# FFN bias rows of a fused attention and FFN kernel: loaded at the start and turned into columns among the first key transposes

## The chip, the cores and the metric

One Trainium2 chip, one of its cores. The metric is the device time in microseconds (us) of one execution. All runs used here are of the fast state, with a granted TensorE clock of 1.0 (in the kernel before and the changed one it is lower only past 1235 us, when PE has finished). The engines are called PE (TensorE, with PEld for its weight loads), DVE (VectorE), ACT (ScalarE), POOL (GpSimd) and SP (SyncE).

## The reference, cut to what matters

```python
xn = _layernorm(A_x)                                   # 2048 rows of 512
s  = attention(xn @ wq, k_cache, v_cache) @ wo         # 32 heads, 2048 keys of 128
h  = jnp.einsum("bsd,df->bsf", xn, w1) + b1            # F = 1792; b1 is the bias of this change
g  = silu(relu(h)**2 @ w2 + b2)
out = A_x + s * g
```

The kernel computes `h` transposed, with the 1792 features on the partitions: 14 chunks of 128. The bias must then be a column for each chunk, a tile `b1f` of 128 x 14, while it lies in memory as 14 rows of 128.

## The kernel before

Each engine has its own list of instructions, which wait on semaphores; in the traces here it starts them in the order of its list (an example: in k_late_keys_changed below the bias rows land near 6.3 us, but their transpose stands behind the keys and starts at 7.60 us). PE does in each step (there are 8 to a head and block of 512 queries, 1024 in all) two score matmuls into `psA`, one to three "fillers" into `psF`, and eight weighted-value matmuls into `psO`. Fillers are the matmuls of everything else: query projections, FFN, output projection. A filler job is a chain of matmuls that accumulate in one bank; two banks take turns, and a job's bank is free when DVE has evacuated it:

```python
(n, mm, evac), i = cur[0]
bank = bank_no[0]
mm(i, bank)                               # waits for t_bankF[bank] at i == 0
if i == n - 1:
    t_bankF[bank] = evac(bank, step)      # DVE reads the bank
    bank_no[0] ^= 1                       # the next job takes the other bank
```

All jobs are chains of 4 to 16 matmuls, save one: the bias job, a single transpose of 14 rows on PE, with its copy on DVE.

```python
def mm(n, bank):
    box[0] = E(PE, partial(_peT, out=bankF(bank)[:, 0:64].bitcast(BF16)[:, 0:NFC], in_=b1b[:],
                           ident=ident[0:NFC, 0:NFC]), deps=[tok_b1, t_ident, t_bankF[bank]])
def evac(bank, step):
    t_b1[0] = E(DV, partial(_copy, out=b1f[:], in_=...), deps=[box[0]])
    return t_b1[0]
return 1, mm, evac
...
jobs = [(3, 3, job_b1(), None)]           # sorted in behind projections 1 and 2
```

The first head is special: its keys arrive as rows and are transposed on PE, in halves `b`, and its query rows come in four blocks `i`. The order of emission at the start (each engine takes its own instructions from it, in this order):

```python
k0_transpose(0); k0_copy(0); ...; ln_scale(0, 0)
first_transpose(0)     # PE: normalised rows of block 0
k0_transpose(1)        # PE: second half of the keys
k0_copy(1); ...        # ACT
first_copy(0)          # DVE: xnT
first_proj(0)          # PE
ln_scale(0, 1)         # DVE: xn_t of block 1
first_evac(0)          # DVE: qt_sb
first_transpose(1)     # PE
gen_scores(0)          # PE: the first scores
```

The softmax here doesn't subtract the row's maximum and nothing guards it: scores larger than these inputs give would overflow.

Of the kernel before, what the change touches and what calls it, by code (L numbers as in the profile page):

```python
# [7 lines left out]
BF16 = mybir.dt.bfloat16  # L8
F32 = mybir.dt.float32
P = 128  # L10
# [204 lines left out]
def bass_recurrent_scan__mha_block_cached__dense_activation_squared_relu__prompt_kernel(  # L215
# [23 lines left out]
    NFC = F // P  # L239
# [12 lines left out]
    S = _Sched()  # L252
    PE = S.eng("PE")
    AC = S.eng("ACT")
    DV = S.eng("DVE")
    GP = S.eng("POOL")
    SP = S.eng("SP")
    E = S.emit
# [22 lines left out]
    b1b = sb("b1b", [NFC, P], BF16)  # L281
    b1f = sb("b1f", [P, NFC], F32)
# [8 lines left out]
    ident = sb("ident", [P, P], BF16)  # L291
# [7 lines left out]
    psA = nc.alloc_psum_tensor("psA", [P, 4 * 512], F32)  # L299
# [3 lines left out]
    def bankF(i):  # L303
        return psF[:, i * 512:(i + 1) * 512]

    def bankO(i):
        return psO[:, i * 512:(i + 1) * 512]
# [10 lines left out]
    sl_b1 = S.slot("b1")  # L318
# [10 lines left out]
    t_ident = E(GP, partial(_ts, out=ident[:], in0=identf[:], scalar1=0.0, scalar2=None,  # L329
                            op0=ALU.is_equal), deps=[t_idf])  # L330
    t_ones = None
    for i in range(NSL):
        t_ones = E(GP, partial(_memset, out=v_sb[:, i, :, Dh:Dh + 1], val=1.0))


    t_xl = {}
    t_xn = {}
# [18 lines left out]
    def ln_rstd(j, i, n=1, eng=GP):  # L356
        jt = j * TPB + i
        prev = [t_xn.get(jt - TPB), t_xr.get(jt - TPB)]
        t = E(DV, partial(_bn_aggr, out=mv_t[:, i, :], in_=st_t[:, i, 0:6 * n]),
              deps=[t_bn[jt]] + prev)  # L360
        t = E(eng, partial(_ts, out=ve_t[:, i:i + 1], in0=mv_t[:, i, 1:2], scalar1=1.0,
                           scalar2=LN_EPS, op0=ALU.mult, op1=ALU.add), deps=[t] + prev)
        t_xr[jt] = E(GP, partial(_tt, out=rstd[:, i:i + 1], in0=ve_t[:, i:i + 1], in1=mhalf[:],
                                 op=ALU.pow), deps=[t, t_mhalf])
# [5 lines left out]
    def ln_scale(j, i):  # L370
        jt = j * TPB + i
        t_xn[jt] = E(DV, partial(_ts, out=xn_t[:, i, :], in0=x_ln[:, i, :],
                                 scalar1=mv_t[:, i, 0:1], scalar2=rstd[:, i:i + 1],
                                 op0=ALU.subtract, op1=ALU.mult),
                     deps=[t_xr[jt], t_xnr.get(jt - TPB)])
# [12 lines left out]
    t_k0 = [None, None]  # L388
    t_kT0 = [None, None]
    t_q0 = [None] * TPB  # L390
# [21 lines left out]
    def k0_transpose(b):  # L412
        n = NKT // 2
        for c in range(n):
            t_kT0[b] = E(PE, partial(_peT, out=bankO(b).bitcast(BF16)[:, c * P:(c + 1) * P],
                                     in_=kT[:, NSL - 1, (b * n + c) * P:(b * n + c + 1) * P],
                                     ident=ident[:]),
                         deps=[t_k0[b], t_ident], inc=(c == n - 1))

    def k0_copy(b):  # L420
        n = NKT // 2 * P
        t_k0[b] = E(AC, partial(_act, out=kT[:, 0, b * n:(b + 1) * n],
                                in_=bankO(b).bitcast(BF16), func=ACT.Copy), deps=[t_kT0[b]])

    def first_transpose(i):
        for c in range(NDC):
            t_xT[i] = E(PE, partial(_peT, out=bankF(1)[:, 0:256].bitcast(BF16)[:, c * P:(c + 1) * P],
                                    in_=xn_t[:, i, c * P:(c + 1) * P], ident=ident[:]),
                        deps=[t_xn[i], t_ident, tok_xT[0][i - 1] if i else None],
                        inc=(c == NDC - 1))  # L430
        t_xnr[i] = t_xT[i]

    def first_copy(i):
        tok_xT[0][i] = E(
            DV, partial(_copy, out=xnT[:, :, i * P:(i + 1) * P],
                        in_=bankF(1)[:, 0:256].bitcast(BF16).rearrange("p (c q) -> p c q", q=P)),
            deps=[t_xT[i]])

    def first_proj(i):
        for c in range(NDC):  # L440
            t_proj[0] = E(PE, partial(_mm, out=bankF(0)[:, i * P:(i + 1) * P],
                                      lhsT=wq_sb[:, 0, c, :], rhs=xnT[:, c, i * P:(i + 1) * P],
                                      start=(c == 0), stop=(c == NDC - 1)),
                          deps=[t_wqfill[0], tok_xT[0][i], t_q0[i - 1] if i else None],
                          inc=(c == NDC - 1))
# [21 lines left out]
    t_exp = [None] * NPAIR  # L467
# [36 lines left out]
    def gen_scores(pi):  # L504
        g, k = divmod(pi, NPR)
        s2, i = pi % 2, g % NSL
        assert t_kfill[g] is not None and t_evac[g] is not None
        t = None
        if g == 0:
            qt, b = divmod(pi, 2)  # L510
            for c in range(NKT // 2):
                t = E(PE, partial(_mm_shared, out=psA[:, s2 * 1024 + c * P:s2 * 1024 + (c + 1) * P],
                                  lhsT=kT[:, 0, (b * NKT // 2 + c) * P:(b * NKT // 2 + c + 1) * P],
                                  rhs=qt_sb[:, 0, qt * P:(qt + 1) * P], start=True, stop=True),
                      deps=[t_k0[b], t_q0[qt], t_exp[pi - 2] if pi >= 2 else None],
                      inc=(c == NKT // 2 - 1))
        else:
            for n in range(2):
                tt = 2 * k + n
                t = E(PE, partial(_mm, out=psA[:, s2 * 1024 + n * 512:s2 * 1024 + (n + 1) * 512],  # L520
                                  lhsT=kT[:, i, tt * P:(tt + 1) * P], rhs=qt_sb[:, g % NQS, :],
                                  start=True, stop=True),
                      deps=[t_exp[pi - 2] if pi >= 2 else None, t_kfill[g], t_evac[g],
                            t_bankF[0] if pi == 0 else None],
                      inc=(n == 1))
        if k == NPR - 1:
            t_S_last[g] = t
        t_exp[pi] = E(AC, partial(_act, out=pT[:, pi % NPT, :],
                                  in_=psA[:, s2 * 1024:(s2 + 1) * 1024],
                                  func=ACT.Exp, scale=SM_SCALE),  # L530
                      deps=[t, t_PV[pi - NPT] if pi >= NPT else None])
# [51 lines left out]
    t_bankF = [None, None]  # L583
# [19 lines left out]
    def at(step, fn):  # L603
        events.setdefault(step, []).append(fn)

    def job_proj(g):
# [14 lines left out]
                          deps=[t_proj[g], t_S_last[g - NQS] if g >= NQS else None])  # L621
            return t_evac[g]
        return NDC, mm, evac

    t_b1 = [None]

    def job_b1():

        box = [None]

        def mm(n, bank):
            box[0] = E(PE, partial(_peT, out=bankF(bank)[:, 0:64].bitcast(BF16)[:, 0:NFC],
                                   in_=b1b[:], ident=ident[0:NFC, 0:NFC]),
                       deps=[tok_b1, t_ident, t_bankF[bank]])

        def evac(bank, step):
            t_b1[0] = E(DV, partial(_copy, out=b1f[:],
                                    in_=bankF(bank)[:, 0:64].bitcast(BF16)[:, 0:NFC]),
                        deps=[box[0]])
            return t_b1[0]  # L640
        return 1, mm, evac

    def job_h(j, c):
        js = slice(j * QB, (j + 1) * QB)
# [119 lines left out]
                                op=ALU.add), deps=[t, tok_xt[jt]])  # L764


    jobs = [(3, 3, job_b1(), None)]
    for g in range(1, NG):
        jobs.append((NPR * g - 15, NPR * (g - 2), job_proj(g), g))
    for j in range(NQB):  # L770
        b = 30 + j * (SPB - 6)
# [92 lines left out]
    load_w1(0)  # L864
    for i, k in enumerate([2, 3, 12, 18, 26, 34]):
        at(k, partial(load_w1, i + 1))
    tok_b1 = tok_b2 = None

    def load_b1():
        nonlocal tok_b1  # L870
        tok_b1 = S.emit_dma(GP, partial(_dma, out=b1b[:],
                                        in_=B_b1.rearrange("(c p) -> c p", p=P)), sl_b1)

    def load_b2():
        nonlocal tok_b2
# [33 lines left out]
    ln_scale(0, 0)  # L909
    first_transpose(0)  # L910
    k0_transpose(1)
    k0_copy(1)
    t_kfill[0] = t_k0[1]
    ln_rstd(0, 1, eng=DV)
    first_copy(0)
    first_proj(0)
    ln_scale(0, 1)
    first_evac(0)
    first_transpose(1)
    gen_scores(0)  # L920
    ln_bn(0, 2)
    gen_scores(1)
    first_copy(1)
    ln_rstd(0, 2)
    first_proj(1)
    first_evac(1)
    gen_pv(0)
    ln_bn(0, 3, 0, HD)
    gen_scores(2)
    ln_scale(0, 2)  # L930
    first_transpose(2)
    ln_bn(0, 3, HD, D)
    gen_scores(3)
    first_copy(2)
    ln_rstd(0, 3, n=2)
    load_b1()
    first_proj(2)
    first_evac(2)
    gen_pv(1)
# [22 lines left out]
    for pi in range(NPAIR):  # L962
# [4 lines left out]
        n = 0  # L967
# [31 lines left out]
    step = NPAIR  # L999
# [41 lines left out]
```

## Time and profile before

| | before |
|---|---|
| median of three runs | 1239.27 us (1239.21 to 1239.27) |
| span of the profiled run | 1237.5 us |
| PE, ACT, DVE busy | 99%, 85%, 38% |
| waits of PE in the list | 2.0 us, of which 0.4 after the first 20 us |
| bias rows: load issued, used | 12.09 us, 20.40 us |

PE sets the time; its busy share is an upper view, since its records overlap (a 512-column matmul has a record of 0.38 us, but the next starts 0.22 us later). So this document reads starts, not busy sums. Some matmul records are also missing from this trace: PE has 11666 records and PEld 11873, so a small gap in the list of PE isn't always idle time. The lines are shown in the prediction.

### The profile page before, as it was taken

The numbers are of one execution on the slowest core, as the hardware profiler recorded it, in microseconds if no ns is written. First come the engines' busy times: TensorE is split into PE (matmuls) and PEld (weight loads), VectorE is DVE, ScalarE is ACT, GpSimd is POOL, SyncE is SP. The second block draws the span as 40 slices with busy tenths as digits, with TensorE's granted clock in tenths as the row PEclk, the third lists the DMA queues.
The fourth block names the chain that finished last, engine by engine and source line by source line (L and its number), as shares of the span: only waits on it lengthen the run. The fifth ranks groups of instructions, "written<-read, shape, count | busy, mean of one in ns | idle before, by whom it ended". The sixth has DMA issues, their size and how long they took to land.

```text
span 1237.5 us, 26703 instructions
## 1 busy us (share of the span) xinstructions
PE 1221.4 (99%) x11666; PEld 818.6 (66%) x11873; DVE 472.9 (38%) x953; ACT 1053.6 (85%) x1044; POOL 32.0 (3%) x73
## 2 busy tenths in 40 slices
PE   9999999999999999999999999999999999999998
PEld 7666666666666666666666666666666666666666
DVE  4453333244435332334444532233344333324333
ACT  7888888888888888888888888888888888888885
POOL 1010000000002000000000200000000000000000
PEclk9999999999999999999999999999999999999999
DMA  9999988777888787877788888787788788778761
GB/s 209 217 235 180 191 178 140 128 139 140 144 154 166 143 161 133 133 141 146 135 132 169 171 141 142 137 150 137 133 145 149 147 154 157 138 134 146 146 123 31
DMA packets 686868, 185.41 MB, mean 150 GB/s; under 512 B 673536, under 2 KB 685568, under 8 KB 686752
## 3 DMA queue, kind: packets, MB, share of 16 engines
q1 hardware_dynamic: 684656, 179.62, 80.7%
q0 software_dynamic: 1424, 3.81, 1.1%
q8 instruction: 94, 1.54, 0.5%
q10 hardware_dynamic: 672, 0.26, 0.1%
q14 instruction: 22, 0.18, 0.1%
HBM read 96.60 MB, written 2.10 MB: 80 GB/s over the span
## 4 chain that ended last, share of the span: by engine, by line
PE 98%; issue 1%; DVE 1%; DMA 0%; ACT 0%; POOL 0%; DVEq 0%
PE psO L157 38%; PE psA L152 35%; PE psF L152 25%; PE psA L157 0%; DMA x_ln<-in_A_x_dram 0%; DVE out_t L165 0%; PE psF L196 0%; DVE tmp_t L175 0%; ACT pT L161 0%; DVE xnT L179 0%; DVE st_t L200 0%; DVE o_bf L165 0%; DVE qt_sb L179 0%; POOL rstd L165 0%; DVE o_un L179 0%
## 5 line engine op out<-in xcount | busy, mean ns | idle before, releaser
L161 ACT ACTIVATE pT<-psA 128x1024 bf16<-128x1024 f32 x1024 | 1043.6, 1023 | 165.0 <-PE psA L152 119.7
L157 PEld LDWEIGHTS psO<-v_sb,pT 128*128 128x128 bf16 x8192 | 547.9, 98 | 240.8 <-issue 13.1
L157 PE MATMUL psO<-v_sb,pT 128*128 128x129 bf16 x8192 | 631.2, 220 | 0.9 <-ACT pT L161 0.4
L152 PE MATMUL psA<-qt_sb,kT 128*128 128x512 bf16 x1837 | 562.3, 379 | 10.2
L179 DVE COPY o_un<-psO 128x258 f32<-128x258 f32 x256 | 97.4, 422 | 398.5 <-PE psO L157 397.7
L152 PE MATMUL psF<-xnT,wq_sb 128*128 128x512 bf16 (+1 forms) x514 | 167.1, 374 | 0.8 <-DVE b1f L179 0.4
L152 PE MATMUL psF<-wo_all,oT 128*128 128x512 bf16 x479 | 163.4, 379 | 0.1
L152 PEld LDWEIGHTS psA<-qt_sb,kT 128*128 128x128 bf16 x2032 | 156.9, 98 | 0.1
L179 DVE CAST qt_sb<-psF 128x512 bf16<-128x512 f32 (+1 forms) x131 | 88.7, 677 | 103.7 <-PE psF L152 98.0
L152 PEld LDWEIGHTS psF<-xnT,wq_sb 128*128 128x128 bf16 x524 | 50.6, 98 | 60.8 <-issue 1.2
L165 DVE TENSOR_TENSOR o_bf<-o_un,rden 128x512 bf16<-128x512 f32 x128 | 88.5, 692 | 4.7 <-DVE rden L183 0.3
L171 DVE TENSOR_SCALAR r_t<-psF,b1f 128x512 bf16<-128x512 f32 x56 | 42.0, 750 | 116.9 <-PE psF L152 116.9
L152 PEld LDWEIGHTS psF<-wo_all,oT 128*128 128x128 bf16 x480 | 46.9, 98 | 56.4
L152 PE MATMUL psF<-xnT,w_sb 128*128 128x512 bf16 x224 | 77.1, 379 | 0.0
L152 PE MATMUL psF<-w_sb,h2T 128*128 128x512 bf16 x223 | 73.7, 379 | 0.0
L152 PEld LDWEIGHTS psF<-w_sb,h2T 128*128 128x128 bf16 x224 | 21.9, 98 | 26.4
L152 PEld LDWEIGHTS psF<-xnT,w_sb 128*128 128x128 bf16 x224 | 21.9, 98 | 26.4
L165 DVE TENSOR_TENSOR z_t<-psF,b2bc 128x512 f32<-128x512 f32 x16 | 11.1, 692 | 68.3 <-PE psF L152 63.8
L165 DVE TENSOR_TENSOR acc<-psF,acc 128x512 f32<-128x512 f32 x28 | 19.3, 689 | 30.0 <-PE psF L152 30.0
L208 POOL DMA_DIRECT2D out_dram<-out_t x12 | 6.7, 554 | 890.4 <-DVE out_t L165 890.4
L183 DVE RECIPROCAL rden<-o_un 128x4 f32<-128x4 f32 x128 | 22.9, 179 | 4.4
L165 DVE TENSOR_TENSOR h2T<-r_t 128x512 bf16<-128x512 bf16 x56 | 23.8, 425 | 1.9
(44 smaller groups left out, 162.2 us busy)
## 6 DMA issues: line engine op xcount, KB each, us to landing
v_sb<-in_A_v_cache_dram SPq DMA_DIRECT2D x127, 512.0 KB, 4.7
wq_sb<-in_A_wq_dram SPq DMA_DIRECT2D x127, 128.0 KB, 3.4
wo_all<-in_A_wo_dram SPq DMA_DIRECT2D x4, 1024.0 KB, 6.3
w_sb<-in_B_w_dram SPq DMA_DIRECT2D x14, 256.0 KB, 5.1
oT<-o_bf SPq DMA_TRANSPOSE x128, 4.0
x_t<-in_A_x_dram POOLq DMA_DIRECT2D x16, 128.0 KB, 3.2
kT<-in_A_k_cache_dram SPq DMA_TRANSPOSE x127, 4.5
x_ln<-in_A_x_dram SPq DMA_DIRECT2D x15, 128.0 KB, 3.7
```

The lines of the kernel that those rows point to most:

```text
L152: return e.matmul(out, lhsT, rhs, start=start, stop=stop)
L157: return e.matmul(out, lhsT, rhs, start=start, stop=stop, skip_group_check=True)
L161: return e.activation(out, in_, func, bias=bias, scale=scale)
L165: return e.tensor_tensor(out, in0, in1, op)
L171: return e.tensor_scalar(out, in0, scalar1=scalar1, scalar2=scalar2, op0=op0, op1=op1)
L179: return e.tensor_copy(out, in_)
L183: return e.reciprocal(out, in_)
L208: return e.dma_start(out, in_)
```

## The change

The intent is to take the bias job out of the fillers. The rows are loaded at the very beginning; PE transposes them behind the second half of the first keys; DVE copies the columns before it normalises the second block of rows. The target moves from a filler bank to the last bank of `psA`, which the first scores of the kernel then have to leave alone until the copy is done.

```diff
     for i in range(NSL):
         t_ones = E(GP, partial(_memset, out=v_sb[:, i, :, Dh:Dh + 1], val=1.0))
+    tok_b1 = S.emit_dma(GP, partial(_dma, out=b1b[:], in_=B_b1.rearrange("(c p) -> c p", p=P)),
+                        sl_b1)
...
+    def bias_rows():
+        t_b1[0] = E(PE, partial(_peT, out=psA[:, 1536:1600].bitcast(BF16)[:, 0:NFC], in_=b1b[:],
+                                ident=ident[0:NFC, 0:NFC]), deps=[tok_b1, t_ident])
+    def bias_copy():
+        t_b1[0] = E(DV, partial(_copy, out=b1f[:], in_=...), deps=[t_b1[0]])
...
-                      deps=[t_k0[b], t_q0[qt], t_exp[pi - 2] if pi >= 2 else None],
+                      deps=[t_k0[b], t_q0[qt], t_exp[pi - 2] if pi >= 2 else t_b1[0]],
...
-    def job_b1():            # cut: shown above
-    jobs = [(3, 3, job_b1(), None)]
+    jobs = []
...
     k0_transpose(1)
+    bias_rows()
     k0_copy(1)
     ...
     first_copy(0)
+    bias_copy()
     first_proj(0)
     ln_scale(0, 1)
...
-    load_b1()                # was issued behind the fourth block's statistics
```

More of the change, by code (lines that the diff above doesn't have):

```diff
@@ L437, in first_copy @@
             deps=[t_xT[i]])
+    t_b1 = [None]
+    def bias_rows():
+        t_b1[0] = E(PE, partial(_peT, out=psA[:, 1536:1600].bitcast(BF16)[:, 0:NFC], in_=b1b[:],
+                                ident=ident[0:NFC, 0:NFC]), deps=[tok_b1, t_ident])
+    def bias_copy():
+        t_b1[0] = E(DV, partial(_copy, out=b1f[:],
+                                in_=psA[:, 1536:1600].bitcast(BF16)[:, 0:NFC]), deps=[t_b1[0]])
     def first_proj(i):
@@ L623, in job_proj @@
         return NDC, mm, evac
-    t_b1 = [None]
-    def job_b1():
-        box = [None]
-        def mm(n, bank):
-            box[0] = E(PE, partial(_peT, out=bankF(bank)[:, 0:64].bitcast(BF16)[:, 0:NFC],
-                                   in_=b1b[:], ident=ident[0:NFC, 0:NFC]),
-                       deps=[tok_b1, t_ident, t_bankF[bank]])
-        def evac(bank, step):
-            t_b1[0] = E(DV, partial(_copy, out=b1f[:],
-                                    in_=bankF(bank)[:, 0:64].bitcast(BF16)[:, 0:NFC]),
-                        deps=[box[0]])
-            return t_b1[0]
-        return 1, mm, evac
     def job_h(j, c):
@@ L866, in bass_recurrent_scan__mha_block_cached__dense_activation_squared_relu__prompt_kernel @@
         at(k, partial(load_w1, i + 1))
-    tok_b1 = tok_b2 = None
-    def load_b1():
-        nonlocal tok_b1
-        tok_b1 = S.emit_dma(GP, partial(_dma, out=b1b[:],
-                                        in_=B_b1.rearrange("(c p) -> c p", p=P)), sl_b1)
+    tok_b2 = None
     def load_b2():
```

## The prediction

> **What bounds the kernel now.** I read the page from the top: the busy table and the clock row, then the chain that ended last. They say which engine's time is the kernel's time.
>
> ```profile
> PE 1221.4 (99%) x11666; PEld 818.6 (66%) x11873; DVE 472.9 (38%) x953; ACT 1053.6 (85%) x1044; POOL 32.0 (3%) x73
> PEclk9999999999999999999999999999999999999999
> ...
> PE 98%; issue 1%; DVE 1%; DMA 0%; ACT 0%; POOL 0%; DVEq 0%
> ```
>
> TensorE is busy 99% of the span, at full clock, and the chain lies on it for 98%. DVE (38%), ACT (85%) and POOL (3%) have room. So a change pays only where it takes work off TensorE or takes away a wait of TensorE. The list of waits of TensorE is therefore the next view, and it is short:
>
> ```profile
> PE psA L152 <- POOL mhalf L187: 1.0, 1, 1.0
> PE psO L157 <- ACT pT L161: 0.4, 1, 0.4
> PE psF L152 <- DVE b1f L179: 0.4, 1, 0.4
> PE psF L152 <- DVE xnT L179: 0.2, 1, 0.2
> ```
>
> That is 2.0 us of waits in 1237.5 us. One entry, 0.4 us, once, names b1f, the tile that this change moves. It is the only wait of TensorE after the first 20 us, so the whole gain must be found around it. The timeline there:
>
> ```profile
> 19.66 0.59 PE L152 MATMUL psA<-qt_sb,kT 128*128 128x512 bf16 x2
> ...
> 20.09 0.38 PE L152 MATMUL psF<-xnT,wq_sb 128*128 128x512 bf16 x1
> 20.32 0.18 DVE L183 RECIPROCAL rden<-o_un 128x4 f32<-128x4 f32 x1
> 20.40 0.09 PEld L196 LDWEIGHTS psF<-ident,b1b 14*128 14x128 bf16 x1 [0.42 <-issue]
> 20.40 0.18 PE L196 MATMUL psF<-ident,b1b 14*128 14x14 bf16 x1
> 20.51 0.45 PEld L157 LDWEIGHTS psO<-v_sb,pT 128*128 128x128 bf16 x8
> 20.51 0.63 PE L157 MATMUL psO<-v_sb,pT 128*128 128x129 bf16 x8
> 20.53 0.69 DVE L165 TENSOR_TENSOR o_bf<-o_un,rden 128x512 bf16<-128x512 f32 x1
> 20.92 0.15 PEld L152 LDWEIGHTS psA<-qt_sb,kT 128*128 128x128 bf16 x2
> 20.98 0.59 PE L152 MATMUL psA<-qt_sb,kT 128*128 128x512 bf16 x2
> 21.14 0.68 DVE L179 CAST qt_sb<-psF 128x512 bf16<-128x512 f32 x1
> ...
> 21.75 0.16 DVE L179 CAST b1f<-psF 128x14 f32<-128x14 bf16 x1
> ...
> 21.97 0.38 PE L152 MATMUL psF<-xnT,wq_sb 128*128 128x512 bf16 x1 [0.40 <-DVE b1f L179]
> ...
> 22.19 0.61 PE L157 MATMUL psO<-v_sb,pT 128*128 128x129 bf16 x8
> ```
>
> The columns are start, duration, engine, line, operation, tiles. The reader is to see a normal step first: two score matmuls at 19.66, a filler at 20.09, that is 0.43 us from the first score to the filler. The step after it takes 0.99 us from score (20.98) to filler (21.97). DVE works from 20.32 to 21.91 without a gap: reciprocal, normalisation, evacuation of projection 2, then the bias columns.
>
> **What the Trainium skill says.** (1) "TensorE: Matmul & The Clock Gate", Single matmul latency and Back-to-back issue gap: a matmul's own duration includes a drain that the next one overlaps, and a 512-column one follows the last after about 216 ns. The trace agrees: records of 0.38 us follow each other by 0.22 us (two in 0.59 us). So a filler costs the kernel 0.216 us, and I count starts, not durations. (2) "Perfetto Trace Analysis", Transposes and Matmuls: independent groups should rotate through different PSUM banks so that an evacuation overlaps the next group. The fillers rotate over two banks; the trace shows what happens when one group is a single instruction long: the rotation comes back before the evacuation. (3) "DMA: Bandwidth & Descriptors", Anatomy of one DMA and SWDGE vs HWDGE vs iDMA: a DMA issued from GpSimd has a fixed cost of some 2 us, and each DMA engine alternates between the software and hardware queues. The trace has 3.6 us from issue to landing for this very load (at 12.09 us), which I use instead. (4) "PSUM — Partial Sum Buffer", PSUM bank collisions: guard PSUM by bank, not by address. The change puts the bias transpose in psA's last bank and makes the first two score groups wait for its copy; that is this guard. No view of the kernel before can show it.
>
> **The change part by part.**
>
> Removed at 20 us, the slot: the filler before the bias started at 20.09 and would release the engine at 20.09 + 0.22 = 20.31; the weighted values start at 20.51. So the bias transpose costs 0.20 us of TensorE (its 14 columns are cheap; its own weight load was not hidden behind the matmul before it).
>
> Removed at 20 us, the wait: 0.99 - 0.43 = 0.56 us. The view of waits says 0.40 because it begins to count only after the drain of the score matmuls (20.98 + 0.59 = 21.57). Does it go away? Projections 1 and 2 and the bias take banks 1, 0 and 1, so projection 3 needs bank 0, whose evacuation ends at 21.14 + 0.68 = 21.82. The label b1f is only the last DVE record before the start; the real releaser is probably qt_sb. But the cause is still the bias job: it uses up bank 1 in one instruction. Without it, projection 3 gets bank 1, free since its evacuation ended at 17.10, and bank 0 isn't wanted until projection 3 is over, four fillers later (about 23 us). So the wait should vanish, not move. Sum removed: 0.20 + 0.56 = 0.76 us.
>
> Added at the start, TensorE: one transpose between the second half of the key transposes and the first projection. The timeline there:
>
> ```profile
> 6.00 0.61 PE L196 MATMUL psO<-ident,kT 128*128 128x128 bf16 x8
> ...
> 6.20 0.42 DVE L179 COPY xnT<-psF 128x512 bf16<-128x512 bf16 x1 [0.21 <-PE psF L196]
> ...
> 6.65 0.41 DVE L171 TENSOR_SCALAR xn_t<-x_ln,mv_t,rstd 128x512 bf16<-128x512 bf16 x1
> ```
>
> The last key transpose starts near 6.00 + 0.61 - 0.22 = 6.39, and the projection can't start before 6.77, because it waits for the copy xnT, which ends at 6.62. The bias transpose (0.18 us alone) falls in that hole: 0 us, if its data are there.
>
> Added at the start, the load: POOL is free after its small memsets at about 2.13 us and next has work at 4.69; the issue takes 0.74 us, so it disturbs nothing there. Landing: 2.13 + 3.6 = 5.7 us, against 6.4 us when TensorE wants it. The margin is 0.7 us, with the DMA engines filled by the first keys and values.
>
> Added at the start, DVE: the copy b1f (0.16 us by itself) goes between xnT and the second normalisation xn_t (6.65). DVE has no hole there, so xn_t, the transposes after it (7.12) and the first scores (7.63) move by some 0.1 to 0.16 us. The chain runs through these scores and from there through TensorE, so I count 0.12 us on the path.
>
> Moved: one filler job less. Every later filler stands one place earlier and on the other bank. The total of TensorE work is otherwise the same, and TensorE waits for nothing after 22 us, so I count 0.
>
> Sum: -0.20 - 0.56 + 0.12 = -0.64 us, so 1239.27 - 0.64 = 1238.63, rounded to 1238.6 us.
>
> **The rivals.** (a) The load lands late. TensorE runs in order, so it would then stand in front of the first projection with nothing to do. For it: at that time two 256 KB key loads and four 128 KB rows are in flight, and software loads of more bytes took up to 4.8 us (b2bc). 2.13 + 4.8 = 6.9, a stall of about 0.5 us, which eats most of the gain: 1239.1 us. Against it: 3.5 KB, and an own queue. I give it one in four. (b) The wait is handed on. If DVE's pile-up (o_un, rden, o_bf, qt_sb) rather than the bank order decides, then some TensorE instruction waits at about 21 to 22 us anyway, and only the slot is won: 1239.27 - 0.20 + 0.12 = 1239.2 us. Against it: no other head of the 128 shows this wait, with the same DVE pile-up. One in eight. (c) The shifted fillers meet the evacuations at the end of a head in new phases and waits of some 0.2 us appear in places: up to 1239.5 us. Against it: in the kernel before all phases occur over the run and none waits. (d) The start costs nothing, the copy hiding behind other waits: 1238.5 us.
>
> **Range and chances.** Most of the weight lies on 1238.5 to 1238.8; rivals (a) to (c) pull upwards to 1239.5; a cheaper start and a luckier filler order pull to 1238.0. The three runs of before differ by 0.06 us, so the noise doesn't widen it much. Range 1238.0 to 1239.5. All of the mechanism is worth under 0.1% of the time, and no rival comes near 2% (25 us): within 2% 0.99, faster 0.005, slower 0.005.
>
> **What would show it.** Right: the wait of psF on b1f is gone from the list of waits; the step from score to filler near 21 us takes 0.43 us; the bias matmul stands at about 6.4 to 6.7 us without idle time before the projection; the first 512-column step at 17.24 comes 0.1 us later; the idle of ACT at 23.27 (0.64 us) shrinks. Wrong: a wait of PE for b1b's DMA at 6.5 us, a new psF wait in the body, or the start of the first scores later than 7.9 us. The prediction falls if the time is above 1239.5 or below 1238.0.

## The result and the profile after

The changed kernel took 1238.82 us (median of 6 runs, 1238.69 to 1238.93), the kernel before 1239.28 us in the same rounds (1239.21 to 1239.48). The ratio is 0.9996 with a 95% interval of 0.9983 to 1.0009: the same time. Ratios here are the mean time of one kernel's fast runs over that of the other's of the same rounds, so not quite the ratio of the medians. The interval is wider (over 1 us each way) than anything this change does; the traces are finer than the times, and the argument rests on them.

The busy table and the chain of the changed kernel:

```profile
PE 1231.6 (100%) x11873; PEld 818.2 (66%) x11873; DVE 472.5 (38%) x953; ACT 1053.8 (85%) x1044; POOL 31.9 (3%) x73
...
PE 99%; DVE 0%; DMA 0%; ACT 0%; issue 0%; POOL 0%; DVEq 0%
```

PE seems 10 us busier than before. It is not: all 11873 matmuls are recorded here, and 207 were missing before. The waits of PE, in the same view as before (total, times, longest; the first line, the wait for POOL's memset, is unchanged and left out):

```profile
PE psO L157 <- ACT pT L161: 0.4, 1, 0.4
PE psO L196 <- DMA kT<-in_A_k_cache_dram: 0.4, 1, 0.4
PE psF L196 <- DVE xn_t L171: 0.3, 1, 0.3
```

The wait of psF on b1f is gone, and no new wait stands in the body. Two new ones stand in the first 8 us: the key transposes for their load, and the row transposes for xn_t. This list is of PE alone; the weight load (PEld) of the bias transpose also waits, for the DMA of the bias rows:

```profile
6.77 0.09 PEld L196 LDWEIGHTS psA<-ident,b1b 14*128 14x128 bf16 x1 [0.18 <-DMA b1b<-in_B_b_dram]
```

The bias transpose starts 0.64 us after the key transposes here, and 0.54 or 0.55 us after them in the six other traces that have this order, so this wait is worth 0.09 us. The timeline of PE at 20 us:

```profile
19.86 0.59 PE L152 MATMUL psA<-qt_sb,kT 128*128 128x512 bf16 x2
20.30 0.59 PE L152 MATMUL psF<-xnT,wq_sb 128*128 128x512 bf16 x2
20.73 0.62 PE L157 MATMUL psO<-v_sb,pT 128*128 128x129 bf16 x8
21.18 0.59 PE L152 MATMUL psA<-qt_sb,kT 128*128 128x512 bf16 x2
21.61 0.38 PE L152 MATMUL psF<-xnT,wq_sb 128*128 128x512 bf16 x1
```

Two fillers follow each other at 20.30 where one filler and the bias transpose stood; and from the score at 21.18 to the filler at 21.61 it is 0.43 us, as in any other step, where it was 0.99 us.

**The body.** To separate start and rest, I take the time from the first 512-column score group (near 17 us, where the regular steps begin) to the start of the last run of matmuls. Both ends are starts of PE instructions. Before, they are 17.24 us and

```profile
1228.62 5.86 PE L152 MATMUL psA<-wo_all,oT 128*128 128x512 bf16 x58
```

so 1211.38 us; in the changed kernel 17.45 us and

```profile
1228.05 5.86 PE L152 MATMUL psA<-wo_all,oT 128*128 128x512 bf16 x58
```

so 1210.60 us. The body is 0.78 us shorter, and the start 0.21 us longer (17.24 to 17.45). The sum, 0.57 us, is the difference of the two ends. These two numbers explain the times: in all twelve traces of this document, the time of the traced run less its first 512-column start and its body is 10.64 to 10.69 us.

**The start.** The chain that ended last, between 5.7 and 8.5 us (start, duration, what). Before:

```profile
5.76 0.41 PE psF L196 x4
...
6.20 0.43 DVE xnT L179
...
6.77 0.38 PE psF L152 x4
7.15 0.37 PE psF L196 x4
...
7.63 0.62 PE psA L157 x8
```

It goes from the row transposes through DVE's copy xnT and the first projection to the first scores. In the changed kernel:

```profile
6.14 0.62 PE psO L196 x8
...
6.78 0.19 PE psA L196
...
6.99 0.17 DVE b1f L179
7.16 0.33 DVE xn_t L171
...
7.54 0.40 PE psF L196 x4
7.94 0.51 PE psA L157 x8
```

It now goes from the row transposes (5.74 us) through the key transposes, the bias transpose, the bias copy and the second normalisation. (The chain cuts overlapping matmuls where one hands over to the next; the first scores start at 7.83 us. The end of DVE's evacuation qt_sb, 7.68 us, fits as their releaser too; it also stands behind xn_t on DVE.) The new guard of the first scores doesn't bind: the bias copy ends at 7.16 us. This path is the part of the result which was not foreseen, and the second set of experiments is about it.

### The profile page after: what moved, and what is told of

Its sections match the earlier page's. It is cut to its first block, busy times and chain, and to the rows that moved or that the text cites. A ratio compares the mean times of both kernels' runs of the same rounds, so it can differ in the third digit from the quotient of the medians.

```text
span 1236.9 us, 26910 instructions
## 1 busy us (share of the span) xinstructions
PE 1231.6 (100%) x11873; PEld 818.2 (66%) x11873; DVE 472.5 (38%) x953; ACT 1053.8 (85%) x1044; POOL 31.9 (3%) x73
## 4 chain that ended last, share of the span: by engine, by line
PE 99%; DVE 0%; DMA 0%; ACT 0%; issue 0%; POOL 0%; DVEq 0%
PE psO L157 38%; PE psA L152 36%; PE psF L152 25%; PE psA L157 0%; DMA x_ln<-in_A_x_dram 0%; DVE out_t L165 0%; PE psF L196 0%; DVE tmp_t L175 0%; ACT pT L161 0%; DVE xn_t L171 0%; DVE st_t L200 0%; PE psO L196 0%; POOL rstd L165 0%; DVE xnT L179 0%; DVE mv_t L204 0%
## 5 line engine op out<-in xcount | busy, mean ns | idle before, releaser
L152 PE MATMUL psA<-qt_sb,kT 128*128 128x512 bf16 x2032 | 604.4, 379 | 0.0
L152 PE MATMUL psF<-xnT,wq_sb 128*128 128x512 bf16 (+1 forms) x524 | 169.8, 374 | 0.1
```

The source lines that it names most:

```text
L152: return e.matmul(out, lhsT, rhs, start=start, stop=stop)
```

## The experiments

Ten kernels ran, all with correct results. The times are all "same" by the interval, so each is read by its trace; medians are given for completeness. "Body" is as above.

### Why the body is shorter: four runs

The theory, A: the bias job uses up a bank in a single instruction, so the next job wants the other bank before DVE has evacuated it. Rivals: the load came too late (R1); the order of later fillers is luckier (R2); PE really waits for the bias copy, as the label in the view of waits says (R3).

**d1_early_load_only**: the kernel before with the early load and nothing else.

```diff
+    tok_b1 = S.emit_dma(GP, partial(_dma, out=b1b[:], ...), sl_b1)   # behind the memsets
-    load_b1()
```

> The kernel before with only the load of the bias rows moved to the beginning; transpose and copy stay a filler near 20 us. Theory A (the filler that is one instruction long uses up a PSUM bank, so the next filler meets the other bank before its evacuation): the load has no part in it, so the wait of psF near 22 us stays (0.40 us in the list of waits, 0.99 us from score to filler) and the time is that of before, 1239.3 us. Rival R1 (the late load, issued at 12.09 us, is what makes the fillers wait): the wait goes and the time is 1238.6 to 1238.8 us. It also shows what the early load alone does to the start: if it delays the first key loads, the first scores come later than 7.63 us and the key transposes wait for their load as in the changed kernel (first at 5.04); if not, they stand at 7.6 and 4.8.

Measured: body 1211.37 us, the wait of 0.40 us on b1f unchanged, 1239.40 us against 1239.36. R1 falls: when the rows arrive has nothing to do with it. At the start the key transposes did wait for their load (5.25 and 6.39 us), though this kernel has no bias transpose there; and the first scores waited for the evacuation qt_sb:

```profile
7.71 1.05 PE L157 MATMUL psA<-qt_sb,kT 128*128 128x128 bf16 x16 [0.25 <-DVE qt_sb L179]
```

**d2_dummy_filler_with_copy**: the changed kernel with a useless one-instruction filler where the bias job was.

```diff
-    jobs = []
+    jobs = [(3, 3, job_dummy(), None)]   # transpose b1b into bankF(bank), DVE copies it to a spare tile
```

> The changed kernel with a useless filler put back where the bias job was: the same small transpose into the filler bank and a copy on DVE to a tile that nobody reads. Theory A: the whole loss near 20 us comes back, 0.20 for the slot and 0.56 for the wait, on top of the changed start: 1238.82 + 0.76 = 1239.6 us, score to filler 0.99 us near 21 us. Rival R2 (the gain comes from the shifted order or phase of all later fillers being luckier): the order is that of before again, so the time is also back at 1239.6, but the wait of 0.4 us is not, and the loss lies somewhere after 25 us. The start is that of the changed kernel: first scores at 7.83 us if the delay there is systematic.

Measured: body 1211.38 us, exactly that of before, with a wait of 0.40 us on the spare tile's copy near 22 us. That wait is what R2 did not expect. By the step near 22.6 us, 0.57 of the 0.78 us is already there (from the first 512-column score to that step's scores it is 22.59 - 17.19 = 5.40 us here, 22.28 - 17.45 = 4.83 us in the changed kernel), and d4 below accounts for the other 0.21 us; so nothing is left for the order of the later fillers, and R2 falls. The time was 1239.23 us, 0.4 below the expectation: 0.26 us of it is an early start (first 512-column score at 17.19 us, not 17.45), and 0.11 us is that the expectation began from the median of 1238.82 us, while the traced run of the changed kernel took 1238.71 us.

**d3_dummy_filler_no_copy**: the same, without the copy.

```diff
         def evac(bank, step):
-            return E(DV, partial(_copy, out=b1s[:], ...), deps=[box[0]])
+            return t_bankF[bank]
```

> As the last, but the useless filler has no copy on DVE; it still passes the turn to the other bank. Theory A: the next projection still wants bank 0, whose evacuation by DVE ends at about 22.0 us, so the wait stays, 0.3 to 0.5 us in the list of waits and now named after qt_sb: 1239.5 to 1239.6 us. Rival R3 (the wait is for the bias copy on DVE, as the view of waits labels it): no copy, no wait, only the slot of 0.20 us is lost: 1239.0 us.

Measured: body 1211.37 us. The wait is still there, and now has another name; the timeline of PE:

```profile
21.18 0.59 PE L152 MATMUL psA<-qt_sb,kT 128*128 128x512 bf16 x2
22.18 0.38 PE L152 MATMUL psF<-xnT,wq_sb 128*128 128x512 bf16 x1 [0.40 <-DVE qt_sb L179]
```

Without any bias copy, the wait is the same 0.40 us. So b1f was only the last DVE record before the start; PE waited for qt_sb, the evacuation of bank 0; it starts 0.15 us after the end of qt_sb before (21.82 to 21.97) and 0.16 us after it here (22.02 to 22.18). R3 falls. The time was 1239.47 us, about as expected.

**d4_dummy_filler_no_turn**: the same, but the useless filler leaves the turn with its own bank.

```diff
         def evac(bank, step):
+            bank_no[0] ^= 1
             return t_bankF[bank]
```

> As the last, but the useless filler hands the turn back, so that the next projection writes the same bank 1 after it, and nothing is copied. Theory A: no wait, only the slot: 1238.82 + 0.20 = 1239.0 us, score to filler 0.43 us near 21 us. If the wait of some 0.5 us stays (1239.5 us), the bank order isn't the cause but DVE's pile-up or the switch between the small transpose and a matmul.

Measured: no wait, body 1210.81 us, 1238.79 us (0.2 below the expectation; the traced run had an early start as in d2). The timeline of PE:

```profile
20.91 0.59 PE L152 MATMUL psA<-qt_sb,kT 128*128 128x512 bf16 x2
21.34 0.38 PE L152 MATMUL psF<-xnT,wq_sb 128*128 128x512 bf16 x1
```

The step is back at 0.43 us with the same work on DVE as in d3. Between d3 and d4 only the turn of the bank differs: 1211.37 - 1210.81 = 0.56 us is the wait. Between d4 and the changed kernel only the slot differs: 1210.81 - 1210.60 = 0.21 us.

### Why the start moved: six runs

The four traces above showed a pattern. Below, "statistics" is the start of the first row statistics (the moment the first rows have landed, 3.38 to 3.50 us), "keys" the start of the second half's key transposes and "scores" the start of the first scores, both counted from the statistics; "keys to scores" is their difference.

| kernel | bias between keys and xn_t | keys | scores | keys to scores | body |
|---|---|---|---|---|---|
| before | no | 2.50 | 4.13 | 1.63 | 1211.38 |
| d1 | no | 2.97 | 4.29 | 1.32 | 1211.37 |
| changed | yes | 2.67 | 4.36 | 1.69 | 1210.60 |
| d2 | yes | 2.50 | 4.13 | 1.63 | 1211.38 |
| d3 | yes | 2.77 | 4.38 | 1.61 | 1211.37 |
| d4 | yes | 2.50 | 4.13 | 1.63 | 1210.81 |
| s1 | yes | 2.49 | 4.12 | 1.63 | 1210.60 |
| changed again | yes | 2.50 | 4.13 | 1.63 | 1210.60 |
| s2 | no | 2.86 | 4.18 | 1.32 | 1210.59 |
| s3 | no | 2.61 | 4.17 | 1.56 | 1210.60 |
| late keys, changed | yes | 3.64 | 5.24 | 1.60 | 1210.60 |
| late keys, holes | no | 4.04 | 5.36 | 1.32 | 1210.60 |

The theory, A2: the change ties DVE to the first key load. PE runs in order, so the bias transpose stands behind the keys; DVE runs in order, so xn_t stands behind the bias copy (in the late changed kernel below xn_t starts at 7.91 us, right behind b1f at 7.82, though POOL's rstd for it is ready near 6.5); and the scores stand behind the transposes of xn_t. Rivals: two more instructions simply cost their own time wherever they stand (R4); the bias rows land late (R5).

**s2_bias_in_the_holes**: the transpose goes behind the second row transposes into a free part of the filler bank, the copy into a hole of DVE.

```diff
-    bias_rows()              # behind k0_transpose(1)
-    bias_copy()              # behind first_copy(0)
...
     first_transpose(1)
+    bias_rows()              # out=bankF(1)[:, 256:320]
...
     ln_rstd(0, 2)
+    bias_copy()
                             # cut: the waits changed to match; the guard of the first scores goes
```

> The changed kernel with the bias transpose after the second row transposes (in the filler bank's free half) and its copy in the hole of DVE before the second evacuation (0.45 us idle at 8.9). Theory A2 (in the changed kernel the bias ties DVE to the first key load: key load, key transposes, bias transpose, copy, xn_t, all in order, which costs nothing when the keys land by 5.95 us and some 0.2 us when they land at 6.1 to 6.3): here xn_t starts at 6.6 whenever the keys land, the first scores at 7.55 to 7.65, or 7.7 if the keys land as late as 6.4. The body (from the first 512-column score to the last run of matmuls) is 1210.60 us as in the changed kernel, the time 1238.5 to 1238.7 us. Rival R4 (the two instructions cost their own time, about 0.1 us, wherever they stand in the start): 7.7 or later and 1238.8 us.

Measured: the keys were late (2.86), the scores at 4.18 nonetheless (7.66 us), xn_t at 6.63 us, body 1210.59 us, 1238.57 us against 1239.25. This is as A2 says: with keys later than in d3, the scores are 0.20 us earlier. R4 expected 7.7 or more, which 7.66 misses by little; the table is stronger: keys to scores is 1.32 us here, with the two instructions, and 1.32 us in d1, which doesn't have them there. So R4 falls in the form "wherever they stand" (but see the reading of the table).

**s3_columns_by_dma**: no transpose, no copy; GpSimd loads the columns with a converting load of single elements.

```diff
-    tok_b1 = S.emit_dma(GP, partial(_dma, out=b1b[:], ...), sl_b1)
-    bias_rows()
-    bias_copy()
...
     ln_rstd(0, 3, n=2)
+    t_b1[0] = S.emit_dma(GP, partial(_dma_slow, out=b1f[:], in_=B_b1.rearrange("(c p) -> p c", p=P)), sl_b1)
```

> No bias transpose and no copy at all: a cast load of two-byte elements from GpSimd at about 12 us writes the columns. Theory A2: the start is that of the kernel before, scores at 7.55 to 7.65, body 1210.60 us, time 1238.5 to 1238.7 us. Risk: 1792 descriptors of one element; if they take longer than the 16 us until the columns are wanted near 28 us, or hold up GpSimd's rstd or the rows behind them, the body shows a wait of DVE and then of TensorE.

Measured: issued at 12.1 us (1.29 us of POOL), landed 5.5 us later, first used at 26.6 us; scores at 4.17, body 1210.60 us, 1238.64 us. The risk did not come true: no wait in the body.

**s1_load_on_act_queue**: the changed kernel with the rows loaded from ACT instead of POOL.

```diff
-    tok_b1 = S.emit_dma(GP, ...)         # behind the memsets
     fill_wq(0, AC)
+    tok_b1 = S.emit_dma(AC, partial(_dma, out=b1b[:], ...), sl_b1)
```

> The changed kernel with the bias rows loaded through ACT's hardware queue instead of GpSimd's. Rival R5 (it is the late landing of the bias rows, 6.78 us in the changed kernel's trace, that moves the first scores from 7.63 to 7.83): rows there by 5.5 us, bias transpose right behind the key transposes without a wait, scores at 7.65, 1238.6 us. Theory A2: with the keys on time (by 5.95) 7.57, with the keys at 6.1 to 6.3 still 7.75 to 7.83, whatever the bias rows do; 1238.6 to 1238.9 us.

Measured: the keys were on time in this run (5.93 us), scores at 7.56, 1238.61 us. Both theories expect that, so this run decides nothing. What decides against R5 is d3: there the rows landed 4.3 us after an issue near 1.98, so near 6.3 us, long before their transpose at 6.77 us, and the scores were as late (4.38) as in the changed kernel's first trace, where the rows landed only near 6.78 us (4.36). At most 0.06 to 0.09 us of that trace is theirs: 1.69 from keys to scores against 1.60 to 1.63 in the other rows with "yes".

**a_changed_again**: the changed kernel, unedited.

> The changed kernel once more, for a second look at its start and for times of the same rounds as the variants. Theory A2: scores at 7.57 if the second half of the keys is transposed from 5.95 us or before, at 7.75 to 7.85 if from 6.1 to 6.3; body 1210.60 us in both cases; 1238.8 us.

Measured: keys on time (2.50), scores at 4.13, 7.51 us; body 1210.60 us; 1238.40 us against 1239.25, so 0.4 below the expected 1238.8. The same kernel, with its scores 0.23 us earlier (counted from the statistics) than in its first trace, as A2 says.

**k_late_keys_changed** and **k_late_keys_holes**: until here the keys were late in some traces and not in others, for a reason that the edits don't show. These two make them late on purpose, in the changed kernel and in s2.

```diff
-    load_k0(1)
     ...
     ln_load(0, 3, SP)
+    load_k0(1)
```

> The changed kernel with the load of the second half of the first keys issued after the two row loads behind it, so some 0.9 us later, on purpose. Theory A2: the bias transpose stands behind those keys on TensorE, its copy waits on DVE and xn_t behind it, so the first scores come about 4.6 to 5.0 us after the first row statistics (4.13 with the keys on time) and 0.2 to 0.3 us later than in the next kernel. Rival R4: no more than 0.1 us later than the next.

> The same late keys in the kernel that has the bias in the holes. Theory A2: xn_t stays where it was (3.15 us after the first row statistics begin), only TensorE's own order moves: first scores 0.2 to 0.3 us earlier than in the kernel before this one; the body is 1210.6 us in both, so the time differs by the same amount.

Measured: scores at 5.24 and 5.36, so the holes were later, not earlier as expected, and in time nearly equal (1239.50 and 1239.36 us). The expectation took for granted that the keys would land at the same moment; their transposes started 0.40 us apart (3.64 and 4.04). It also had xn_t at 3.15 in the holes; it came at 3.27. From the keys on, which is what A2 is about, it is 1.60 us in the changed kernel and 1.32 us in the other: 0.28 us, in the range expected. The chain of the changed form:

```profile
7.05 0.62 PE psO L196 x8
7.67 0.12 PE psA L196
...
7.82 0.17 DVE b1f L179
7.99 0.33 DVE xn_t L171
```

and of the one with the bias in the holes:

```profile
7.48 0.62 PE psO L196 x8
8.10 0.24 PE psF L152 x4
...
8.36 0.30 DVE qt_sb L179
```

The first goes through bias transpose, copy and normalisation; the second straight from the keys to the projection and its evacuation.

**Reading the table.** Without the bias in the path, keys to scores takes 1.32 us where the keys decide (three rows). With keys at 2.50 that chain would end at 2.50 + 1.32 = 3.82, but the scores come at 4.13, because the other chain (xnT, projection, evacuation) is longer: by this sum, an estimate from the table, the key chain has 0.31 us of slack. With the bias in the path it takes 1.60 or 1.61 us where the keys decide (late keys, d3), which just fills that slack: 2.50 + 1.61 = 4.11, still before 4.13, no cost. (The 1.63 us of the rows with keys on time is set by the other chain.) By the same estimate each 0.1 us by which the keys are later costs about 0.1 us, until the keys decide in the old form too (at about 2.8), and from there the cost is 0.28 us. Of the six traces with the bias in the path and the loads in their usual order, four had the keys on time (2.49 or 2.50) and two had not.

Where the 0.28 us sit can be read from the starts. From the keys to the first projection it is 0.46 us in d1, s2 and the late holes, and 0.66 us in d3 and the late changed kernel. From there to its evacuation qt_sb it is 0.42 or 0.43 us against 0.51 or 0.52 us, and from qt_sb to the scores 0.42 to 0.44 us in all five. So about 0.20 us is the bias transpose itself, standing on PE between the keys and the projection, and only about 0.09 us is DVE, which is still busy with b1f and xn_t when the projection is done. A2 named the second way alone. That the transpose costs its own time once the keys decide is R4's share of the truth. No run moved only one of the two instructions, so this split is read from the traces and not tested.

**A better version?** s2 and s3 can't be told from the changed kernel in time: 1238.57, 1238.64 and 1238.40 us in the same rounds, against 1239.25. They have the shorter body and no coupling, so they should be steadier; five runs each don't show that.

## Why the prediction was right

The time, 1238.82 us, and the later 1238.40 us lie in its range, and the mechanism that it named for the gain near 20 us was the one.

- **The slot**, 0.20: measured 0.21.
- **The wait**, 0.56: measured 0.56. Its two readings hold: the view of waits understated it (0.40, since it begins to count after the last record's drain), and the label b1f was not the releaser.
- **"The wait should vanish, not move"**: it vanished. The rival that some instruction near 21 us waits anyway falls with the changed kernel itself, where DVE does the same reciprocal, normalisation and evacuation (20.52 to 22.03 us) and PE does not wait.
- **The shifted fillers**, 0: measured 0. Body and single costs close to 0.01 us.
- **The start**, 0 for TensorE and +0.12 for the copy on DVE: the step that failed. The prediction said that xn_t and the first scores "move by some 0.1 to 0.16 us" and that "the chain runs through these scores". With the keys on time xn_t did move (counted from the statistics, from 3.15 to 3.35 us in d2), but the scores did not (4.13 in both). They start 0.14 to 0.16 us after the end of qt_sb in all twelve traces, and qt_sb starts at 3.69 in both (d1's line above names it). So with the keys on time the term is 0.00. In the two traces with late keys the scores came 0.23 and 0.25 us later than the 4.13 of before: there the bias transpose no longer fell into a hole of TensorE, and the first projection came 0.15 and 0.16 us later (3.42 and 3.43, not 3.27); DVE added 0.09 us. The prediction did not see that both the transpose and the copy hang on the key load. That its 0.12 lies between the two cases is luck.
- **The landing of the rows**: it worked with 3.6 us, taken from 12 us into the run; at the start it was 4.1 to 4.9 us from POOL, near 6.1 to 6.9 us instead of 5.7. Its rival of a late load was nearer than thought, but the row load cost only 0.09 us in one trace; the rest came with the key load.
- **Its signs**: the wait on b1f is gone, the step takes 0.43 us, and ACT's idle time of 0.64 us is gone. The first 512-column step came 0.21 us later and not 0.1. One sign of "wrong" came true in part: TensorE's weight load waited for b1b's DMA, 0.18 us at 6.77 us.

What stays open: whether the early bias load itself makes the keys late. Keys were on time in four and late in four of the eight traces that have an early bias load and the usual order; of the two without it, one was on time (before, 2.50) and one slightly late (s3, 2.61). That is too few. In the twelve traced runs start and body account for the time to 0.05 us; that the spread of all times of one kernel (1239.19 to 1239.84 us for the kernel before in one set) also comes from the landing of the first loads is only argued, since most timed runs leave no trace.

## What to carry to other kernels

A job that is much shorter than its neighbours in a rotation of buffers costs more than its own time: here 0.21 us of work brought 0.56 us of waiting, because the turn came back before the other bank was evacuated; give it a place outside the rotation. Handing the turn back (d4) also removed the wait, but there the job had nothing to evacuate; with the bias copy the next job would have to wait for that copy before it writes the same bank, and this was not tried. The label in a view of waits can be just the last record before the start, as here; compare the ends of all candidates with it, or take the labelled one away and see whether the wait stays. When something small is put into an idle hole of an engine, ask what it waits for and who stands behind it: a hole is free only as long as what feeds it is on time.

## What the Trainium skill lacked or had wrong

- "DMA: Bandwidth & Descriptors", Anatomy of one DMA: its fit (about 2.0 us fixed, plus bytes over 436e3) gives 2.0 us for the 3.5 KB of bias rows from GpSimd. Measured from issue to landing: 3.6 us at 12 us into the run, 4.1 to 4.9 us in the first 7 us among the large loads. Its table of latencies says that an HBM access is slower at high load, but no page gives the spread of landing times, which mattered here: the second half of the first keys could be transposed between 2.49 and 2.97 us after the first row statistics, in kernels that load it the same way.
- "TensorE: Matmul & The Clock Gate", Back-to-back issue gap: it gives about 131 ns for a 512-column matmul in a sustained stream of weight loads and matmuls, and calls 216 ns the isolated gap, while the same page's Step-by-step: what each phase is for gives 216 ns for back-to-back matmuls. The traces side with the latter: the stream itself runs at 216 ns (16 fillers in a row take 3.62 us: 3.62 less one record of 0.38, over 15). The prediction named the first section for the 216 ns; the figure was right, the section was not.
- The same page, PE-mode transpose: it gives 275 to 390 ns for a transpose and says that the full clock does not engage for it. Here the eight 128 x 128 transposes of the second key half take 0.61 or 0.62 us in every trace, with records of 0.22 us, so they follow each other by 57 ns, about as fast as the ordinary 128-column matmuls of the first scores (16 in 1.05 us, 55 ns). Those of the first half took 0.62 to 1.04 us. A 14-row transpose behind a filler matmul costs 0.21 us of PE (d4 against the changed kernel), which no page states.
- "Perfetto Trace Analysis", Matmuls: it advises rotating over PSUM banks, but no page says that the groups in a rotation of two should be of similar length; a group of one instruction cost 0.56 us here.
